# Routed experts with exact-split products: gate scaling on ScalarE, low weight parts on VectorE

## The chip, the cores and the metric

The kernel runs on one core of a Trainium2 chip. The metric is the device time of one execution in microseconds, as a median over runs. The core has five engines: PE (TensorE, matrix products), DVE (VectorE), ACT (ScalarE), POOL (GpSimd) and SP (SyncE, which here only issues DMAs). ACT and POOL issue DMAs too. Every engine works through its own instructions in their order.

## The reference, cut to what matters

Three layers follow each other over 2 x 768 tokens of width 512. The first is a retention attention of 8 heads. The second picks one of 8 experts for each token and scales the expert's output by its gate `p[e]`; the third is a gated layer with a convolution of three taps.

```python
# layer 2, for each token
h = np.maximum(x[b, s] @ w1[e], 0.0)
out[b, s] = p[e] * (h @ w2[e])
# layer 3
h = np.maximum(x @ w_in, 0.0)
conv_out += conv_w[k][None, None, :] * hp[:, k:k + S, :]
gate = 1.0 / (1.0 + np.exp(-conv_out))
return (h * gate @ w_out).astype(np.float32)
```

Inputs are float32 but for the third layer's weights, which the kernel decodes from 64 bit.

## The kernel before, in words

**Split products.** Each large product is computed as three float32r products, high x high, high x low and low x high. A weight piece of 128 x 1024 is called a unit. `split_first` (L180) has ACT round it to `whi` (L186); `split_second` (L189) has an engine that its caller names compute `wlo = raw - whi` (L194), and then has SP issue the load of a further unit into the freed `raw` buffer (there are four). `whi` and `wlo` have ten buffers each, so `whi` of a new unit waits until PE has used up an old one. 64 units belong to the experts. Eight more are the third layer's weights (`wdec`); the default of `split_unit` (L198) gives the low parts of the last four of these to POOL.

**Decoding.** `dec_first` and `dec_second` (L258, L272) decode the third layer's weights between the experts, 16 pieces in all: ACT reads the loaded piece `draw` (L226, L227), DVE does five operations (L229 to L235), POOL two (L237, L238), then the load of another piece is issued, on POOL's queue in the experts' loop (L255).

**The order around the change** is the order in which the code is written (a manual schedule), engine by engine. The stages are:

- The attention over twelve chunks, until about 91 us. Eight units are split here, on DVE.
- `alone(0, 0)`: the first 128 rows of expert 0, mixed with the end of the routing (`route_blocks`, `route_rest`); two units are split by a call at L831. `T(0, (1,))` (L638 to L644) transposes the second 128 rows: PE, then ACT (`xsh`), then DVE (`xsl`, L644).
- `alone(0, 1)`: the other rows of expert 0; two units are split by L715 and four by the default.
- Experts 1 to 6: `L1(e)` (first product, L763; ACT `hh` L768, DVE `hl` L769), `T(e + 1)`, one or two units by the default, `L2(e)` (second product, L792). `L1` splits a unit behind each of its steps `dt` = 0, 1 and 2 (L774) and finishes a decoding at `dt` = 0 and starts one at `dt` = 2. `L2` splits a unit behind each of its four steps `j` (L796), finishes a decoding at `j` = 1 and starts one at `j` = 3.
- Expert 7 in two halves (`alone(7, 0)`, `alone(7, 1)`). In the second half the outputs of batch 0 are gathered by index (`c_gather`, POOL's indirect DMA, tiles `yg`), scaled by the gate (`c_scale`, L989) and transposed and split (`c_T`: PE L995 into `x2p`, ACT high part L1005, DVE low part L1008), between the steps of the product L729.
- `moe2`: `h2(c, f0, f1)` computes groups of 12 products (L1038) into one of three PSUM banks. `conv` takes a bank through ACT `hs` (L1052) and `cs` (L1055), DVE `cs` twice (L1057), ACT `sg` (L1061), POOL `sg` (L1062), ACT `gh` (L1066) and DVE `gl` (L1067). `o2(c)` computes the output products (L1090), ACT copies them out (L1104). Between `h2(0)` and the four groups of `h2(1, 0, 4)` stand the six scalings of batch 1.

Of the kernel before, what the change touches and what calls it, by code (L numbers as in the profile page):

```python
# [13 lines left out]
AF = mybir.ActivationFunctionType  # L14
ALU = mybir.AluOpType
# [79 lines left out]
def tile_kernel(ctx: ExitStack, tc: tile.TileContext, consts, q, k, v, w_gate, w_local, w1, w2, w_in, conv_w, w_out, out):  # L95
# [565 lines left out]
    def moe(mo):  # L661
# [25 lines left out]
        def alone(e, half, free):  # L687
# [16 lines left out]
            for f in range(2):  # L704
                pb = bank_b("l1t")
                fs = slice(f * 512, (f + 1) * 512)
                for dt in range(KD):
                    wh, wl = split[e * 8 + dt]
                    for n, (a, b_) in enumerate(((xh, wh), (xh, wl), (xl, wh))):
                        nc.tensor.matmul(pb, lhsT=a[:, dt, :], rhs=b_[:, fs], start=(dt == 0 and n == 0),  # L710
                                         stop=(dt == KD - 1 and n == 2))
                    if f and free:
                        split.pop(e * 8 + dt)
                        if dt % 2 == 0:
                            split_unit(nc.vector if e else nc.gpsimd)  # L715
                    if f and dt == 1:
                        back(0)
                    if dt < KD - 1:
                        yield
                hr[f] = mo.tile([P, 512], F32, name="hr", tag="ow", bufs=2)  # L720
                nc.scalar.activation(out=hr[f], in_=pb, func=AF.Relu)
                yield
# [25 lines left out]
        def L1(e):  # L748
            xh, xl = xs_t.pop(e)
            hh, hl = h_tiles(e)  # L750
            pb = [bank_b("l1") if j < 3 else bank_d("l1") for j in range(KF // 2)]
            for dt in range(KD):
                wh, wl = split[e * 8 + dt]
                if dt == 0:
                    dec_second(nc.gpsimd)
                elif dt == 2:
                    dec_first(mo)
                for ft in range(KF):
                    o = pb[ft // 2][:, (ft % 2) * CAP:(ft % 2 + 1) * CAP]
                    fs = slice(ft * P, (ft + 1) * P)  # L760

                    for n, (a, b_) in enumerate(((wh, xh), (wl, xh), (wh, xl))):
                        nc.tensor.matmul(o, lhsT=a[:, fs], rhs=b_[:, dt, :], start=(dt == 0 and n == 0 and ft % 2 == 0),  # L763
                                         stop=(dt == KD - 1 and n == 2), skip_group_check=True)
                    if dt == KD - 1 and ft % 2:
                        fp = ft // 2
                        dst = hh[:, 2 * fp:2 * fp + 2, :].rearrange("p a t -> p (a t)")
                        nc.scalar.activation(out=dst, in_=pb[fp], func=AF.Relu)  # L768
                        nc.vector.scalar_tensor_tensor(out=hl[:, 2 * fp:2 * fp + 2, :].rearrange("p a t -> p (a t)"),  # L769
                                                       in0=pb[fp], scalar=0.0, in1=dst.bitcast(F32), op0=ALU.max,  # L770
                                                       op1=ALU.subtract)
                split.pop(e * 8 + dt)
                if dt < KD - 1:
                    split_unit(nc.gpsimd if dt == 0 else nc.vector)  # L774

        def L2(e):
            hh, hl = h_t.pop(e)
            yp = [bank_c(f"y{t}") for t in range(2)]

            for j in range(KF // 2):  # L780
                wh, wl = split[e * 8 + KD + j]
                if j == 1:
                    dec_second(nc.gpsimd)
                elif j == 3:
                    dec_first(mo)
                for jj in range(2):
                    ft = 2 * j + jj
                    ws = slice(jj * DM, (jj + 1) * DM)
                    for part in (((hh, wh), (hh, wl)), ((hl, wh),)):
                        for t in range(2):  # L790
                            for a, b_ in part:
                                nc.tensor.matmul(yp[t], lhsT=a[:, ft, t * P:(t + 1) * P], rhs=b_[:, ws],  # L792
                                                 start=(ft == 0 and a is hh and b_ is wh),
                                                 stop=(ft == KF - 1 and a is hl))
                split.pop(e * 8 + KD + j)
                split_unit(nc.gpsimd if j == 0 else nc.vector)  # L796
            for t in range(2):
                ys = mo.tile([P, DM], F32, name="ys", tag="ys", bufs=2)
                nc.scalar.copy(ys, yp[t])
                r = YROW + e * CAP + t * P  # L800
                nc.scalar.dma_start(out=scr[r:r + P, :], in_=ys)
# [25 lines left out]
        for n, _ in enumerate(first):  # L827
            if n in (1, 4):
                next(blocks, None)
            if n in (3, 5):  # L830
                split_unit(nc.gpsimd)  # L831
            if n >= 5:
                next(rest, None)
            if n == 5:
# [151 lines left out]

    def c_scale(t):
        y = yg_t[t]
        nc.vector.tensor_scalar(y, y, G_all[:, t:t + 1], None, op0=ALU.mult)  # L989

    def c_T(b, c):
        y = yg_t.pop(b * NC + c)
# [259 lines left out]
```

## Time and profile before

| what | value |
|---|---|
| median of 3 runs | 463.89 us (463.18 to 464.21) |
| the profiled execution: its time | 462.48 us |
| its span, first to last instruction | 460.7 us |
| PE busy | 421.1 us, 91% |
| DVE busy | 318.1 us, 69% |
| ACT busy | 244.3 us, 53% |
| POOL busy | 212.3 us, 46% |

The profile is of one execution. Its span leaves out 1.78 us at the ends, and its time lies 1.41 us under the median. Positions such as "at 113.7" are microseconds from the start of the span. A row of the timeline has start and length, the engine, the line, what is written and read, how many instructions are merged, and in brackets how long the engine was idle before and what ended that. An instruction's length counts from its start at the engine and holds what it waits there for a port. Busy time of PE holds modelled ends, so for PE the idle gaps and the distances between starts say more than the share.

### The profile page before, as it was taken

The numbers are of one execution on the slowest core, as the hardware profiler recorded it, in microseconds if no ns is written. First come the engines' busy times: TensorE is split into PE (matmuls) and PEld (weight loads), VectorE is DVE, ScalarE is ACT, GpSimd is POOL, SyncE is SP. The second block draws the span as 40 slices with busy tenths as digits, with TensorE's granted clock in tenths as the row PEclk, the third lists the DMA queues.
The fourth block names the chain that finished last, engine by engine and source line by source line (L and its number), as shares of the span: only waits on it lengthen the run. The fifth ranks groups of instructions, "written<-read, shape, count | busy, mean of one in ns | idle before, by whom it ended". The sixth has DMA issues, their size and how long they took to land.

```text
span 460.7 us, 7610 instructions
## 1 busy us (share of the span) xinstructions
PE 421.1 (91%) x2899; PEld 366.3 (80%) x2899; DVE 318.1 (69%) x540; ACT 244.3 (53%) x450; POOL 212.3 (46%) x159
## 2 busy tenths in 40 slices
PE   7899788678999989899998989948998999999996
PEld 4888677555698978789897977738996988998986
DVE  3366888857398969596979887475897263896160
ACT  2445564523575666456565565336866344784341
POOL 4631263306446576757676755384654030353030
PEclk9999999999899999999999999988999999999999
DMA  9989995433386868677778631040220101000101
GB/s 194 216 219 278 303 256 182 143 135 115 113 299 229 287 228 296 219 276 249 275 236 301 238 138 48 29 132 23 68 70 21 49 0 63 7 2 2 68 0 70
DMA packets 56521, 70.00 MB, mean 152 GB/s; under 512 B 28693, under 2 KB 35349, under 8 KB 56482
## 3 DMA queue, kind: packets, MB, share of 16 engines
q1 hardware_dynamic: 45490, 45.75, 32.8%
q0 software_dynamic: 3856, 13.13, 9.0%
q10 hardware_dynamic: 7136, 10.60, 6.5%
q8 instruction: 24, 0.39, 0.3%
q14 instruction: 15, 0.12, 0.1%
HBM read 58.99 MB, written 10.49 MB: 151 GB/s over the span
## 4 chain that ended last, share of the span: by engine, by line
PE 34%; DVE 29%; DMA 14%; POOL 9%; ACT 6%; issue 6%; ACTq 0%; SPq 0%; POOLq 0%; DVEq 0%
PE op L1090 11%; PE h L1038 9%; DVE wlo L194 6%; DMA draw<-in_moe_w_out_dram 6%; POOL wdec L238 3%; POOL dmf L237 3%; DVE cs L1057 3%; DVE gl L1067 3%; DVE dmf L229 2%; DVE hl L769 2%; DMA draw<-in_moe_w_in_dram 2%; PE l1t L710 2%; DMA k<-in_k_dram 2%; DVE xsl L644 2%; ACT whi L186 2%
## 5 line engine op out<-in xcount | busy, mean ns | idle before, releaser
L194 DVE TENSOR_TENSOR wlo<-raw,whi 128x1024 fp32r<-128x1024 f32 x48 | 77.0, 1622 | 21.1 <-ACT whi L186 21.0
L186 ACT CAST whi<-raw 128x1024 fp32r<-128x1024 f32 x64 | 67.1, 1052 | 38.1 <-PE y L792 19.7
L1062 POOL TENSOR_TENSOR sg<-sg,hs 128x384 f32<-128x384 f32 x32 | 37.0, 1158 | 80.2 <-ACT sg L1061 80.1
L1057 DVE SCALAR_TENSOR_TENSOR cs<-hs,cw,cs 128x384 f32<-128x384 f32 x64 | 43.9, 687 | 28.9 <-ACT cs L1055 27.8
L763 PE MATMUL l<-xsl,whi 128*128 128x256 f32 x192 | 54.4, 283 | 0.0
L763 PE MATMUL l<-xsh,wlo 128*128 128x256 f32 x192 | 54.3, 283 | 0.0
L763 PE MATMUL l<-xsh,whi 128*128 128x256 f32 x192 | 54.3, 283 | 0.0
L194 POOL TENSOR_TENSOR wlo<-raw,whi 128x1024 fp32r<-128x1024 f32 x16 | 41.8, 2619 | 26.2 <-ACT whi L186 18.8
L1038 PE MATMUL h<-x,whi 128*128 128x386 f32 x256 | 51.2, 338 | 0.0
L1038 PEld LDWEIGHTS h<-x,whi 128*128 128x128 f32 x256 | 45.2, 189 | 0.2
L237 POOL TENSOR_TENSOR dmf<-dmf,ds 128x512 f32<-128x512 f32 x13 | 23.9, 1842 | 38.6 <-DVE ds L235 38.6
L1090 PE MATMUL op<-whi,gh 128*128 128x512 f32 (+1 forms) x104 | 39.7, 381 | 1.5 <-ACT os L1104 1.5
L792 PE MATMUL y<-whi,hh 128*128 128x512 f32 x96 | 38.6, 402 | 2.1 <-ACT hh L768 2.1
L1090 PE MATMUL op<-whi,gl 128*128 128x512 f32 (+1 forms) x104 | 39.4, 379 | 0.1
L1090 PE MATMUL op<-wlo,gh 128*128 128x512 f32 (+1 forms) x104 | 39.2, 377 | 0.0
L792 PE MATMUL y<-wlo,hh 128*128 128x512 f32 x96 | 38.1, 397 | 0.0
L763 PEld LDWEIGHTS l<-xsh,whi 128*128 128x128 f32 x192 | 36.8, 192 | 0.2
L763 PEld LDWEIGHTS l<-xsh,wlo 128*128 128x128 f32 x192 | 36.8, 192 | 0.2
L1067 DVE TENSOR_TENSOR gl<-sg,gh 128x384 fp32r<-128x384 f32 x32 | 33.8, 1055 | 4.6 <-ACT gh L1066 4.6
L763 PEld LDWEIGHTS l<-xsl,whi 128*128 128x128 f32 x192 | 36.8, 192 | 0.0
L792 PE MATMUL y<-whi,hl 128*128 128x512 f32 x96 | 30.5, 400 | 3.8 <-DVE hl L769 3.8
L1038 PE MATMUL h<-x,wlo 128*128 128x386 f32 x128 | 27.7, 337 | 0.0
(200 smaller groups left out, 950.0 us busy)
## 6 DMA issues: line engine op xcount, KB each, us to landing
raw<-in_moe_w_dram SPq DMA_DIRECT2D x64, 512.0 KB, 4.4
scr<-ys ACTq DMA_DIRECT2D x16, 256.0 KB, 3.2
draw<-in_moe_w_out_dram POOLq DMA_DIRECT2D x8, 512.0 KB, 4.8
q<-in_q_dram SPq DMA_DIRECT2D x12, 256.0 KB, 4.5
v<-in_v_dram SPq DMA_DIRECT2D x12, 256.0 KB, 4.8
k<-in_k_dram SPq DMA_DIRECT2D x11, 256.0 KB, 4.4
scr<-xo ACTq DMA_DIRECT2D x11, 256.0 KB, 3.6
out_dram<-os ACTq DMA_DIRECT2D x11, 256.0 KB, 2.0
```

Source lines behind the costliest of these rows:

```text
L186: nc.scalar.copy(hi, raw[u])
L194: engine.tensor_tensor(out=lo, in0=t, in1=hi.bitcast(F32), op=ALU.subtract)
L229: ve.tensor_scalar(mag, mag, F64_LOW, F64_HIGH, op0=ALU.max, op1=ALU.min)
L237: nc.gpsimd.tensor_tensor(out=f, in0=f, in1=s.bitcast(F32), op=ALU.mult)
L238: nc.gpsimd.tensor_tensor(out=out, in0=f, in1=a.bitcast(F32), op=ALU.add)
L763: nc.tensor.matmul(o, lhsT=a[:, fs], rhs=b_[:, dt, :], start=(dt == 0 and n == 0 and ft % 2 == 0), stop=(dt == KD - 1 and n == 2), skip_gr ...
L792: nc.tensor.matmul(yp[t], lhsT=a[:, ft, t * P:(t + 1) * P], rhs=b_[:, ws], start=(ft == 0 and a is hh and b_ is wh), stop=(ft == KF - 1 an ...
L1038: nc.tensor.matmul(pb[:, 0:WN], lhsT=split[u_in + dt][wi][:, fs], rhs=x_[dt // 2][:, dt % 2, :], start=(n == 0), stop=(n == 3 * KD - 1))
L1057: nc.vector.scalar_tensor_tensor(out=cs, in0=tap[j], scalar=cw[:, j, ft:ft + 1], in1=cs, op0=ALU.mult, op1=ALU.add)
L1062: nc.gpsimd.tensor_tensor(out=sg, in0=sg, in1=tap[1], op=ALU.mult)
L1067: nc.vector.tensor_tensor(out=gl, in0=sg, in1=gh.bitcast(F32), op=ALU.subtract)
L1090: nc.tensor.matmul(ops[t][:, 0:n_], lhsT=a[:, ts_], rhs=b_[:, ws], start=(ft == 0 and n == 0), stop=(ft == KF - 1 and n == 2))
```

## The change

The five edits name another engine. Four calls of `split_unit` that gave the low part to POOL now give it to DVE: L715 (expert 0 alone had POOL), L774 (`dt` = 0), L796 (`j` = 0) and L831. `c_scale` is now an ACT activation with a scale taken from a column of `G_all`.

```diff
@@ alone, L715
-                            split_unit(nc.vector if e else nc.gpsimd)
+                            split_unit(nc.vector)
@@ L1, L774
-                    split_unit(nc.gpsimd if dt == 0 else nc.vector)
+                    split_unit(nc.vector)
@@ L2, L796
-                split_unit(nc.gpsimd if j == 0 else nc.vector)
+                split_unit(nc.vector)
@@ between the steps of alone(0, 0), L831
-                split_unit(nc.gpsimd)
+                split_unit(nc.vector)
@@ c_scale, L989
-        nc.vector.tensor_scalar(y, y, G_all[:, t:t + 1], None, op0=ALU.mult)
+        nc.scalar.activation(out=y, in_=y, func=AF.Copy, scale=G_all[:, t:t + 1])
```

PE and SP have the same instructions in the same order as before. On DVE in `alone(0, 0)`, where the block counts (L599 to L603) and the rows of the gathered outputs (L613) are computed:

```order
 L602 SCALAR_TENSOR_TENSOR inc<-nb,small_zero 128x8
 L603 CAST novi<-inc 128x1
+L194 TENSOR_TENSOR wlo<-raw,whi 128x1024
 L613 TENSOR_TENSOR rows<-OH,C 128x96
 L614 TENSOR_REDUCE posf<-rows 128x12
```

A low part now stands ahead of L613; another stands ahead of L599.

On DVE in experts 1 to 6, behind the two `xsl` of `T(e + 1)` and into `L2` (the five operations from L229 on are a decoding), before:

```order
L644 TENSOR_TENSOR xsl<-xsp,xsh 128x4x128 x2
L194 TENSOR_TENSOR wlo<-raw,whi 128x1024 x2
L229 TENSOR_SCALAR dmf<-dmf 128x512
L230 TENSOR_SCALAR dmf<-dmf 128x512
L232 TENSOR_SCALAR ds<-draw 128x512
```

and now:

```order
L644 TENSOR_TENSOR xsl<-xsp,xsh 128x4x128 x2
L194 TENSOR_TENSOR wlo<-raw,whi 128x1024 x3
L229 TENSOR_SCALAR dmf<-dmf 128x512
L230 TENSOR_SCALAR dmf<-dmf 128x512
L232 TENSOR_SCALAR ds<-draw 128x512
```

The low part of the unit split at `j` = 0 stands ahead of the decoding. It stood on POOL, ahead of L237, and is gone from there, as is the one of `L1` behind the load of `draw`.

On ACT in `alone(7, 1)`, where ACT has the high parts of the decoded weights (L186) and of the transposed outputs (L1005):

```order
 L701 CAST hh<-hTp 128x4x128
+L989 ACTIVATE yg_3598<-yg_3598,G_all 128x512
 L186 CAST whi<-wdec_84 128x1024
+L989 ACTIVATE yg_3598<-yg_3598,G_all 128x512
+L989 ACTIVATE yg_3599<-yg_3599,G_all 128x512
 L1005 CAST x_3608<-x2p 128x2x128
 L1005 CAST x_3609<-x2p 128x2x128
 L186 CAST whi<-wdec_85 128x1024
```

Three scalings now stand on ACT ahead of the first pair of L1005; three more follow between the later ones.

On ACT between `h2(0)` and `h2(1, 0, 4)`:

```order
 L1061 ACTIVATE sg<-cs 128x384
 L1066 CAST gh<-sg 128x384
+L989 ACTIVATE yg<-yg,G_all 128x512 x6
 L1052 ACTIVATE hs_3786<-h_4005 128x386
 L1055 ACTIVATE cs<-hs_3786,cw 128x384
```

The six scalings of batch 1 stand ahead of the `hs` that empties the ninth group's bank.

## Rows read from the trace of the kernel before

**Rows 1.** Stretches, experts 1 and 3, sum of six: length, busy by engine, clock.

```profile
130.86:154.19 23.33, 23.33 (x153) 21.40 (x152) 20.33 (x25) 13.92 (x20) 12.29 (x8) 1.00 0.78 284
...
179.40:206.63 27.23, 25.34 (x153) 22.27 (x152) 21.65 (x24) 14.85 (x21) 18.95 (x12) 0.94 0.72 244
...
sum 148.85, PE 142.97 PEld 129.07 DVE 125.70 ACT 88.26 POOL 94.44; mean PE 23.83 PEld 21.51 DVE 20.95 ACT 14.71 POOL 15.74
```

**Rows 2.** Timeline of PE, expert 3: first product of L2 behind a gap.

```profile
193.84 0.50 PE L792 MATMUL y<-whi,hh 128*128 128x512 f32 x1 [1.89 <-ACT hh L768]
```

**Rows 3.** Chain that ended last, around expert 5's L2: start, length, what.

```profile
240.97 2.92 DVE wlo L194
...
248.74 2.56 DVE dmf L229
...
257.74 6.10 DMA draw<-in_moe_w_out_dram
```

**Rows 4.** Timeline of POOL, then DVE, in the same place.

```profile
240.50 2.42 POOL L194 TENSOR_TENSOR wlo<-raw,whi 128x1024 fp32r<-128x1024 f32 x1
...
247.94 3.06 POOL L194 TENSOR_TENSOR wlo<-raw,whi 128x1024 fp32r<-128x1024 f32 x1 [1.76 <-ACT whi L186]
...
258.80 0.41 DVE L229 TENSOR_SCALAR dmf<-dmf 128x512 f32<-128x512 f32 x1
```

**Rows 5.** Low parts by engine: count, shortest/median/longest in ns.

```profile
L194 DVE TENSOR_TENSOR wlo<-raw,whi x48: 1207/1222/3040, 43.6 to 278.1; 128x1024 fp32r<-128x1024 f32 x48
L194 POOL TENSOR_TENSOR wlo<-raw,whi x16: 2372/2440/3062, 109.6 to 272.9; 128x1024 fp32r<-128x1024 f32 x16
```

**Rows 6.** Timelines at 107 to 116 (DVE, POOL, ACT, PE); stretch with its clock.

```profile
109.20 5.24 DVE L613 TENSOR_TENSOR rows<-OH,C 128x96 f32<-128x96 f16 x1
...
109.57 4.74 POOL L194 TENSOR_TENSOR wlo<-raw,whi 128x1024 fp32r<-128x1024 f32 x2
...
107.28 1.99 ACT L186 CAST whi<-raw 128x1024 fp32r<-128x1024 f32 x2
...
115.59 0.50 PE L710 MATMUL l1t<-whi,xsl 128*128 128x512 f32 x1 [1.85 <-DVE xsl L644]
...
116.00:119.60 3.60, 3.60 (x11) 2.57 (x10) 1.78 (x9) 0.66 (x2) 0.00 (x0) 0.53 0.50 190
```

**Rows 7.** Timelines at 305 to 321 (DVE, POOL, PE, ACT).

```profile
304.98 5.45 DVE L989 TENSOR_SCALAR yg<-yg,G_all 128x512 f32<-128x512 f32 x1 [1.56 <-DMA yg<-scr,posi]
...
305.50 4.64 POOL L194 TENSOR_TENSOR wlo<-wdec,whi 128x1024 fp32r<-128x1024 f32 x2
...
311.25 1.09 PE L995 MATMUL x2p<-C,yg 128*128 128x128 f32 x4 [6.22 <-DVE x L1008]
...
318.89 0.33 ACTq L742 DMA_DIRECT2D scr<-ys  x1
...
318.43 2.40 POOL L194 TENSOR_TENSOR wlo<-wdec,whi 128x1024 fp32r<-128x1024 f32 x1 [0.96 <-ACT whi L186]
...
319.94 0.76 DVE L1008 TENSOR_TENSOR x<-x2p,x 128x256 fp32r<-128x256 f32 x2 [1.49 <-ACT x L1005]
...
321.12 0.49 ACT L1052 ACTIVATE hs<-h 128x386 f32<-128x386 f32 x1 [1.21 <-DMA scr<-ys]
```

**Rows 8.** Timelines at 317 to 356 (PE, ACT, PE).

```profile
317.41 0.77 PE L1038 MATMUL h<-x,whi 128*128 128x386 f32 x3
...
339.25 0.49 ACT L1052 ACTIVATE hs<-h 128x386 f32<-128x386 f32 x1
...
342.69 0.39 PE L1090 MATMUL op<-whi,gh 128*128 128x512 f32 x1
...
355.51 0.50 PE L1090 MATMUL op<-whi,gh 128*128 128x512 f32 x1 [1.46 <-ACT os L1104]
```

**Rows 9.** Groups on ACT: count, busy us and mean ns, idle before.

```profile
L1055 ACT ACTIVATE cs<-hs,cw 128x384 f32<-128x384 f32 x32 | 19.8, 618 | 1.0
...
L1005 ACT CAST x<-x2p 128x256 fp32r<-128x256 f32 x24 | 7.9, 375 | 16.3 <-DVE x L1008 8.0 <-PE x2p L995 8.0 <-ACT ys L740 0.4
```

## The prediction

> **What bounds the kernel now.** PE is the busiest engine, so I read what PE waits for, stage by stage, and then who makes it wait. First the stretches of experts 1 to 6, each from the first product of one L1 to that of the next [rows 1]. Each expert has the same products. Expert 1 takes 23.33 us with PE busy throughout; that is PE's own pace. The six together take 148.85, which is 148.85 - 6 x 23.33 = 8.9 us more than this pace. Expert 3 is the longest with 27.23, and its mean clock is 0.94.
>
> Then PE's gaps [rows 2]. The largest one stands where L1 of expert 3 ends and L2 begins: PE waits 1.89 for `hh`; three other experts have gaps at the same place, for `hl`. Then the chain of waits, to see who is late [rows 3]. It runs in a loop: a piece `draw` lands, ACT reads it and rounds a unit, DVE takes 2.92 for one low part, then come `hl`, `xsl`, another low part, 2.56 for one L229, the rest of the decoding, POOL's two operations, and the next load of `draw`, which needs 6.10. ACT stands in its order behind that landing, and so do `hh` and, behind the low part, `hl`.
>
> Two lengths in that loop are far too long. A low part needs 1.22 at the median on DVE [rows 5], an undisturbed L229 needs 0.41 [rows 4]. The timeline of POOL tells why: its low part runs from 240.50 to 242.92, and DVE's, which started at 240.97, ends about 1.1 after that. The next one of POOL runs from 247.94 to 251.00, and DVE's L229 ends at 251.3 [rows 3, 4]. So DVE operations like these two, which read their tensors from SBUF, and POOL's exclude each other: one waits until the other is through.
>
> The same is seen at two more places. At 109.20 DVE's L613, 96 elements wide, takes 5.24 because POOL does two low parts from 109.57 on for 4.74; `xsl` stands behind it, PE waits 1.85, and then runs 3.6 us with the clock at 0.53, the lower of the two levels (1.2 GHz) for nearly all of it [rows 6]. At 304.98 a scaling on DVE takes 5.45 behind two low parts of POOL (4.64), and PE waits 6.22 [rows 7]. After the experts PE has one larger gap more, 1.46 at 355.51 [rows 8]; from there to the end it works through.
>
> **The change, part by part.** The rows below are from the profiled execution (462.48, span 460.7), so the sum is made on it; its 1.41 under the median is kept as an offset.
>
> *The two low parts in `alone(0, 0)`.* POOL's 4.74 go. DVE does them in its own order, 2 x 1.22. Their high parts are ready at 109.27 at the latest [rows 6]. DVE then has, from 108.3: a low part to 109.5, five counting operations of some 0.2 (my estimate from their width; they are no wider than L613), the second low part to about 111.7, L613 without the lock some 0.3, three small ones, and `xsl` by about 113. PE asks for it at 113.74, which is 115.59 - 1.85. So the gap goes, and with it the stretch at the low clock, 3.6 x (1 - 0.53) = 1.7. Term A: 1.85 + 1.7 = 3.5 us; bounds 0 (if something else delays `xsl` as much) and 3.6.
>
> *The twelve low parts in experts 1 to 6.* Each costs DVE 1.22 instead of POOL 2.44, so the pair has 1.2 less to share for each. In the loop the one of L1 no longer blocks DVE's last low part: 2.92 becomes 1.22, a saving of 1.7. The one of L2 now stands ahead of the decoding: 2.56 becomes 1.22 + 0.41 = 1.63, a saving of 0.9. The loop takes some 24.8 now: experts 2 to 6 take (148.85 - 23.33)/5 = 25.1 each, of which 27.23 x 0.06/5 = 0.3 is expert 3's clock. It comes to 24.8 - 2.6 = 22.2. That is under PE's 23.33, so PE sets the pace. The extra low part in L1 lies in a stretch where DVE waits for ACT, and costs nothing as long as DVE has 1.2 us there: it is busy 20.33 of 23.33 in expert 1, its waits for POOL included, and 20.33 + 2 x 1.22 = 22.8 still fits. The freed `raw` buffers are released earlier, because they no longer stand behind L237, L238 and the issue of `draw` on POOL; SP's loads follow them. Expert 3's gap is the one with `hh` last: it hangs on the landing of `draw` alone, which comes 0.9 earlier, so 1.0 of 1.89 stays, and I keep 0.4 for `hl` behind it. Term B: 8.9 - 1.4 = 7.5 us. Bounds: 8.9, and 2 if the loads of `draw`, now issued among other loads, land later and give the rest back.
>
> *The first six scalings, on ACT.* No scaling of this size is seen on ACT. The nearest row is L1055, the same form over 384 columns, 0.62; for 512 columns the bounds are 0.62 and 0.62 x 512/384 = 0.82, and I take 0.7, between them. The Trainium skill ("Perfetto Trace Analysis", Optimizing Scalar/DVE Operations) speaks against this edit: an operation that both engines can do is faster on DVE where a performance mode exists, and ACT is for when DVE is saturated. By that rule the sum would lose 12 x 0.2 us here; the trace differs at 304.98, where the scaling on DVE takes 5.45. On ACT the third scaling can start when its gather has landed, at 304.96 to 304.98 [rows 7]. POOL keeps the four low parts of decoded weights, but no scaling stands behind them. The DVE low parts L1008 read PSUM and one tensor in SBUF; these are not blocked now: a pair at 319.94 takes its usual 0.76 while POOL's low part runs from 318.43 to 320.83 [rows 7]. PE then no longer waits 6.22, and ACT becomes the limit of this stage. From 305.0 it has four scalings (2.8), three high parts of 1.0 [rows 6], ten casts L1005 at 7.9/24 = 0.33 [rows 9], some 0.5 for four very small ones and 0.4 for `ys`: 10.0. So the store of `ys` is issued at 315.0 instead of 318.89, 3.9 earlier, and the first `hs` of the third layer, which waits for that store [rows 7], starts 3.9 earlier.
>
> *The second six scalings, on ACT.* DVE loses them, but ACT gets 6 x 0.7 = 4.2 exactly ahead of the ninth `hs`, now at 339.25 [rows 8]. That `hs` frees the bank for PE's twelfth group (three banks). It would start at 339.25 - 3.9 + 4.2 = 339.55 and end at 340.04. The twelfth group starts now at 342.69 - 2.11 = 340.58 (twelve groups from 317.41, where the stage starts, to 342.69), so it starts 0.5 earlier than now, and PE, which is 3.5 or more ahead by then, waits about 3 us. Such a gap is followed by the low clock (1.85 was), which costs another 1.7. The 48 products from 342.69 then end about 1.2 later than now, in the place of the gap of 1.46, which goes. Term C: 0.3 us gained, or 2.0 if the clock stays up; I take 1.0. Bounds: 4, if ACT is quicker than counted, and -3.6, if the stage before gains nothing (4.2 - 0.85 of slack + 1.7 - 1.46).
>
> Sum: 3.5 + 7.5 + 1.0 = 12.0. Span 448.7, profiled execution 450.5, median 463.9 - 12.0 = **451.9**.
>
> **The rivals.** *The loads decide.* The loop's largest piece is the landing of `draw`, 6.10; if it grows by some 1.5 us for each expert because the weight loads move into it, the loop stays at 24 and term B shrinks to 2 to 3. For it: DMA is busy 0.72 to 0.78 in these stretches [rows 1]. Against it: it is the same number of bytes, and expert 1 keeps PE's pace with 0.78. Time 451.9 + 5 = 457.
>
> *ACT pays for the scalings.* ACT becomes the bound from 305 to 355, the first six scalings gain nothing there, and the second six cost what was worked out: C is -3.6, A and B stand. For it: ACT would stand in its order behind three landings of gathers, and a scaling of 0.7 is longer than one of some 0.5 on DVE. Against it: 6.22 us of idle PE that no longer have a cause. Time 451.9 + 4.6 = 456.5. This is what the rule quoted above from the Trainium skill ("Perfetto Trace Analysis", Optimizing Scalar/DVE Operations) would lead one to expect.
>
> *Slower: DVE behind a late high part.* In L2 DVE now waits for `whi` of `j` = 0 before it decodes, and that `whi` waits for PE to free a buffer. On POOL such a wait held back only POOL (1.76 at 247.94 [rows 4]). The loop is lengthened by whatever `whi` comes later than DVE's `xsl` and low part. It has 23.3 - 22.2 = 1.1 to spare. The kernel is slower as a whole once terms A and C (4.5) are used up too: the experts then take 8.9 + 4.5 = 13.4 more than PE's pace, 2.7 for each of five, and `whi` is 1.1 + 2.7 = 3.8 late in each. At 6 us late the loop takes 28.2 and the time is 463.9 - 4.5 + 5 x 4.9 - 8.9 = 475. In the rows POOL's low part starts at 247.94, before DVE is through with its own (248.7), so `whi` is early, and this is unlikely.
>
> *It doesn't do what it says.* Not all low parts leave POOL: those of the last four decoded units stay, two of them in the 4.64 at 305.50. If the lock held DVE's L1008 too, the gap of 6.22 would stay and term C be -3.6: 456.5.
>
> **How the numbers follow.** The forecast (all three terms near their values) 0.66; loads 0.16; ACT pays 0.08; L1008 locked 0.05; slower 0.05. The best case is 3.6 + 8.9 + 4 = 16.5 gained, 447.4; the range goes from 447.0 to 458.0, which takes in the forecast and most of the three middle cases. A measurement can tell about 0.2% (0.9 us) from no change. Faster by more than that: 0.93, as all but the slower case lie well under 463; within 0.2%: 0.02; slower 0.05.
>
> **What would show it.** A right: L613 under 0.5 and no low clock at 116. B right: each of the six stretches at 23.3 to 24, L229 at 0.4, DVE's low parts near 1.2 with at most an operation of POOL (1.3) in front. B wrong: ACT's L226 still waits for `draw` by 2 us and more. C right: scalings on ACT of 0.6 to 0.8, no gap of 6 us near 305, and a new wait of PE for ACT's `hs` in the twelfth group of L1038. The forecast is wrong if the stretches of the experts stay at 24.9.

## The result, and the profile after

The changed kernel takes 451.07 us (median of 4 runs, 450.61 to 451.4) where the kernel before, run beside it, takes 464.05 (463.18 to 464.6). The ratio is 0.972, interval 0.970 to 0.974: 13.0 us, 2.8%. The forecast was 451.9 with a range of 447.0 to 458.0. The profiled execution took 451.4, its span is 448.9. A run more than 1.5% above the fastest of its kernel counts as slow and is left out where kernels are compared.

I cut both spans at the same products of PE and compare stage by stage (distances between starts, read off PE's timeline):

| stage | before | after | difference | forecast |
|---|---|---|---|---|
| start to the first transposition of `T(0, (1,))` | 109.44 | 111.54 | +2.10 | 0 |
| from there to the first product of expert 1 | 21.42 | 18.65 | -2.77 | A: -3.5 |
| experts 1 to 6 | 148.85 | 139.90 | -8.95 | B: -7.5 |
| start of `alone(7)` to the 49th product of L1090 | 75.80 | 73.74 | -2.06 | C: -1.0 |
| from there to the end | 105.18 | 105.09 | -0.09 | 0 |
| span | 460.69 | 448.92 | -11.77 | -12.0 |

**Who sets the end.** The page's fourth part, the chain of work that ended last, in shares of the span, of before and then of after:

```profile
PE 34%; DVE 29%; DMA 14%; POOL 9%; ACT 6%; issue 6%; ACTq 0%; SPq 0%; POOLq 0%; DVEq 0%
...
PE 59%; ACT 5%; DVE 5%; issue 2%; DMA 2%; POOL 0%; POOLq 0%; ACTq 0%; DVEq 0%
```

**The experts.** The stretches of after that answer to [rows 1], experts 1 and 3 and the sum of six (length, busy by engine, clock, DMA share, GB/s):

```profile
130.19:153.50 23.31, 23.31 (x153) 21.40 (x152) 21.88 (x27) 13.84 (x20) 9.85 (x7) 1.00 0.83 274
...
176.82:200.13 23.31, 23.31 (x153) 21.40 (x152) 21.29 (x25) 14.56 (x20) 13.29 (x10) 1.00 0.80 277
...
sum 139.90, PE 139.90 PEld 128.40 DVE 118.12 ACT 87.96 POOL 68.33; mean PE 23.32 PEld 21.40 DVE 19.69 ACT 14.66 POOL 11.39
```

Expert 3, which took 27.23, now has PE's own pace like the others; the sum of PE's busy time is the sum of the stretches. DVE has twelve low parts more in them and is busy 118.12 instead of 125.70: what it lost in waits is more than what it took over. The low parts and the first step of a decoding, over the whole kernel (count, shortest/median/longest in ns), which answer to [rows 4, 5]:

```profile
L194 DVE TENSOR_TENSOR wlo<-raw,whi x64: 1210/1223/2324, 44.0 to 266.7; 128x1024 fp32r<-128x1024 f32 x64
L229 DVE TENSOR_SCALAR dmf<-dmf x13: 414/420/423, 132.3 to 278.8; 128x512 f32<-128x512 f32 x13
```

The longest L229 is 0.42 now; it was 2.56 in [rows 3]. The longest low part of DVE is 2.32, not 3.04: it waits 1.1 for a POOL operation of the decoding, no longer for a low part.

**Expert 0.** First a row of before, DVE's copy `ys` (L739); then the timelines of DVE and PE of after, where [rows 6] stood:

```profile
117.25 0.36 DVE L739 COPY ys<-y 128x256 f32<-128x256 f32 x1
...
112.38 1.23 DVE L194 TENSOR_TENSOR wlo<-raw,whi 128x1024 fp32r<-128x1024 f32 x1
113.52 0.25 DVE L613 TENSOR_TENSOR rows<-OH,C 128x96 f32<-128x96 f16 x1
...
114.18 0.69 DVE L644 TENSOR_TENSOR xsl<-xsp,xsh 128x512 fp32r<-128x512 f32 x1
...
116.59 0.36 DVE L739 COPY ys<-y 128x256 f32<-128x256 f32 x1
...
118.82 0.50 PE L710 MATMUL l1t<-whi,xsh 128*128 128x512 f32 x1 [0.77 <-ACTq L885]
```

Two stretches of the same place with their clock, the 1.00 ahead of DMA share and GB/s:

```profile
115.00:118.00 3.00, 2.92 (x12) 2.17 (x12) 2.04 (x11) 0.66 (x2) 0.21 (x1) 1.00 0.53 179
118.00:122.00 4.00, 3.23 (x17) 2.57 (x16) 1.10 (x1) 2.78 (x5) 1.68 (x2) 1.00 0.63 196
```

L613 falls from 5.24 to 0.25, `xsl` is there in time, PE's gap of 1.85 is gone, and the clock stays at its upper level (2.4 GHz). But a wait of 0.77 is new, at L885, where the engines read the count of overflow blocks and branch. PE's own branch is long past by then (113.1); it waits until ACT has passed (118.8). ACT comes there behind its store of `ys`, and so behind DVE's L739.

**The scalings.** The timelines of ACT (the third and the fourth scaling) and POOL from 293 on, then of ACT and PE at 325; they answer to [rows 7, 8]:

```profile
293.48 0.72 ACT L989 ACTIVATE yg<-yg,G_all 128x512 f32<-128x512 f32 x1 [0.58 <-DMA yg<-scr,posi]
...
295.58 0.73 ACT L989 ACTIVATE yg<-yg,G_all 128x512 f32<-128x512 f32 x1
...
294.85 4.69 POOL L194 TENSOR_TENSOR wlo<-wdec,whi 128x1024 fp32r<-128x1024 f32 x2
...
306.69 0.49 ACT L1052 ACTIVATE hs<-h 128x386 f32<-128x386 f32 x1 [1.10 <-DMA scr<-ys]
...
324.80 3.78 ACT L989 ACTIVATE yg<-yg,G_all 128x512 f32<-128x512 f32 x6
...
329.01 1.66 PE L1038 MATMUL h<-x,whi 128*128 128x386 f32 x4 [2.56 <-ACT hs L1052]
```

And the stretch behind PE's gap, with its clock of 0.64:

```profile
328.20:332.90 4.70, 3.89 (x14) 3.85 (x15) 3.19 (x5) 4.19 (x10) 1.28 (x2) 0.64 0.00 0
```

The third scaling takes 0.72 instead of 5.45, but it is over before POOL's pair of low parts begins. The fourth and the fifth run beside that pair (294.85 to 299.54) and take 0.73 and 0.74: on ACT they are not held. PE's gap of 6.22 has become gaps of 1.36, 0.76 and 0.86. The six scalings ahead of the ninth `hs` take 3.78, and PE waits 2.56 for that `hs` in the twelfth group.

**Ahead of every edit.** The 2.10 that after loses before 111 is in no term. Two stretches of after show the lower clock (1.2 GHz) there:

```profile
90.00:93.00 3.00, 3.00 (x30) 2.48 (x26) 2.93 (x6) 0.47 (x3) 1.65 (x2) 0.50 0.97 332
100.00:104.00 4.00, 3.99 (x14) 2.72 (x14) 0.52 (x2) 0.92 (x3) 0.00 (x0) 0.57 0.00 0
```

In the profile of before both read 1.00. The instructions are the same up to 110.3, where the first moved low part starts. Not all of the 2.10 is the clock: 0.38 was there by 84, ahead of both stretches. Across the first stretch only 0.07 is added, since PE waited there for 1.43 in before and doesn't now. Across the second, from the product L570 at 99.42 in before (100.01 in after) to the next one of that line, it is 1.40. The last pair of experiments returns to this.

### The profile page after: what moved, and what is told of

It reads as the page before. It is cut to its first block, busy times and chain, and to the rows that moved or that the text cites. A ratio compares the mean times of both kernels' runs of the same rounds, so it can differ in the third digit from the quotient of the medians.

```text
span 448.9 us, 7625 instructions
## 1 busy us (share of the span) xinstructions
PE 420.4 (94%) x2899; PEld 367.5 (82%) x2899; DVE 297.8 (66%) x544; ACT 251.6 (56%) x462; POOL 175.6 (39%) x143
## 4 chain that ended last, share of the span: by engine, by line
PE 59%; ACT 5%; DVE 5%; issue 2%; DMA 2%; POOL 0%; POOLq 0%; ACTq 0%; DVEq 0%
PE l L763 15%; PE y L792 15%; PE op L1090 13%; PE h L1038 9%; PE y L729 2%; DVE cs L1057 2%; DVE gl L1067 2%; PE l1t L710 1%; ACT yg L989 1%; PE xsp L641 1%; DMA scr<-ys 1%; DMA yg<-scr,posi 1%; ACT cs L1055 1%; ACT x L1005 1%; ACT hs L1052 1%
## 5 line engine op out<-in xcount | busy, mean ns | idle before, releaser
L194 DVE TENSOR_TENSOR wlo<-raw,whi 128x1024 fp32r<-128x1024 f32 x64 | 86.8, 1373 | 24.4 <-ACT whi L186 24.3
L186 ACT CAST whi<-raw 128x1024 fp32r<-128x1024 f32 x64 | 66.5, 1054 | 34.6 <-PE y L792 17.4
L237 POOL TENSOR_TENSOR dmf<-dmf,ds 128x512 f32<-128x512 f32 x13 | 26.5, 2042 | 82.7 <-DVE ds L235 59.8
L1038 PE MATMUL h<-x,whi 128*128 128x386 f32 x256 | 52.3, 343 | 2.6 <-ACT hs L1052 2.6
L1090 PE MATMUL op<-whi,gh 128*128 128x512 f32 (+1 forms) x104 | 39.6, 381 | 0.0
L1090 PE MATMUL op<-whi,gl 128*128 128x512 f32 (+1 forms) x104 | 39.4, 379 | 0.1
L1090 PE MATMUL op<-wlo,gh 128*128 128x512 f32 (+1 forms) x104 | 39.2, 377 | 0.0
L792 PE MATMUL y<-whi,hl 128*128 128x512 f32 x96 | 29.6, 389 | 0.0
L669 POOL DMA_INDIRECT xg<-scr,permi x15 | 17.9, 1194 | 25.7 <-ACT hr L721 16.3
```

The costliest lines, as they stand in the source:

```text
L186: nc.scalar.copy(hi, raw[u])
L194: engine.tensor_tensor(out=lo, in0=t, in1=hi.bitcast(F32), op=ALU.subtract)
L237: nc.gpsimd.tensor_tensor(out=f, in0=f, in1=s.bitcast(F32), op=ALU.mult)
L669: nc.gpsimd.indirect_dma_start(out=t, out_offset=None, in_=xrow, in_offset=bass.IndirectOffsetOnAxis(ap=permi[:, col:col + 1], axis=0))
L1038: nc.tensor.matmul(pb[:, 0:WN], lhsT=split[u_in + dt][wi][:, fs], rhs=x_[dt // 2][:, dt % 2, :], start=(n == 0), stop=(n == 3 * KD - 1))
L1090: nc.tensor.matmul(ops[t][:, 0:n_], lhsT=a[:, ts_], rhs=b_[:, ws], start=(ft == 0 and n == 0), stop=(ft == KF - 1 and n == 2))
```

## The experiments

The theory is the prediction's: low parts on POOL lengthen DVE operations, these lengthen the loop through the landing of `draw` and the order of `alone(0, 0)`, and the scalings on ACT are a small part. The main rival is that the scalings carry the gain, or that the loads do. The runs stand on several chips, on which the kernel before has medians of 463.3 to 464.05; a difference from the changed kernel's 451.07 holds to about 0.8.

### One half of the change at a time

Low parts on DVE, the scaling left there:

```diff
-        nc.scalar.activation(out=y, in_=y, func=AF.Copy, scale=G_all[:, t:t + 1])
+        nc.vector.tensor_scalar(y, y, G_all[:, t:t + 1], None, op0=ALU.mult)
```

> The low parts on DVE as in the changed kernel, the twelve scalings left on DVE as before. Theory (three places that add up: the beginning 2.8, the experts' loop 8.9, the scalings 2.1 us): the six stretches of the experts 139.9 in sum, L613 under 0.5, but the third scaling again some 5 us behind POOL's two low parts of decoded weights and PE's gap of 6 us still there; 464.0 - 11.7 = 452.3 us. Rival (the scalings carry the gain, the low parts only move it): 460 or more. Rival (the parts need each other, because a DVE relieved of the scalings is what makes room): stretches of 142 to 146 and 455 to 458.

Measured: 450.86 (450.48 to 451.91), ratio 0.971 (0.967 to 0.975), no different from the whole change. The stretches sum to 141.64, not 139.9 as expected; the time was 1.4 better than expected. The lock is still there for one scaling; timelines of DVE, POOL and PE:

```profile
294.46 0.49 DVE L989 TENSOR_SCALAR yg<-yg,G_all 128x512 f32<-128x512 f32 x1 [1.32 <-DMA yg<-scr,posi]
295.86 4.89 DVE L989 TENSOR_SCALAR yg<-yg,G_all 128x512 f32<-128x512 f32 x1 [0.24 <-DMA yg<-scr,posi]
...
295.78 4.67 POOL L194 TENSOR_TENSOR wlo<-wdec,whi 128x1024 fp32r<-128x1024 f32 x2
...
301.55 1.09 PE L995 MATMUL x2p<-C,yg 128*128 128x128 f32 x4 [4.47 <-DVE x L1008]
```

The third scaling slips in ahead of POOL's pair in 0.49, the fourth arrives 0.08 after the pair's start and takes 4.89. The stage from `alone(7)` to the 49th product of L1090 is 73.24, against 75.80 before and 73.74 with the whole change: there the low parts alone bring as much as the whole change. But no low part of that stage was moved; what differs is when POOL's pair falls against the scalings. In the run below without the loads of `draw`, all low parts are on POOL, and the stage reads 74.49, its gap 4.51.

The scaling on ACT, with all low parts as before (the one line of L989 in the kernel before):

> Only the scalings on ACT, all low parts as before. Theory: the stretches of the experts stay at 148.9 in sum; PE's gap of 6 us near 305 goes, in its place three gaps under 1.5; PE waits 2.5 us for ACT's ninth hs and then runs at the lower clock; 464.0 - 2.1 = 461.9 us. Rival (ACT pays for the scalings): 464 to 468. Rival (the scalings carry the gain): 454 or less.

Measured: 462.35 (459.78 to 464.69), ratio 0.997 (0.995 to 1.000). The stretches of the experts, as a sum:

```profile
sum 149.23, PE 143.12 PEld 129.32 DVE 120.75 ACT 88.23 POOL 93.95; mean PE 23.85 PEld 21.55 DVE 20.12 ACT 14.71 POOL 15.66
```

PE's timeline at the ninth `hs`:

```profile
341.43 1.65 PE L1038 MATMUL h<-x,whi 128*128 128x386 f32 x4 [2.56 <-ACT hs L1052]
```

The experts stay where they were. The gap of 6.22 goes, gaps of 1.43, 0.78, 0.45 and 1.83 come in its place, and 2.56 at the ninth `hs`. By the medians the scalings alone are worth about 1 us, as term C had it; the interval reaches 1.000, so no gain at all isn't excluded.

### The three places of the low parts

The changed kernel with the low part of `L1`'s `dt` = 0 back on POOL:

```diff
@@ L774
-                    split_unit(nc.vector)
+                    split_unit(nc.gpsimd if dt == 0 else nc.vector)
```

> The changed kernel with the low part behind dt = 0 of L1 back on POOL (six of the sixteen). Theory (a loop through the landing of draw, 24.8 us before, PE's pace 23.3): this one blocks DVE's last low part ahead of hl, so the loop loses 1.7 of the 2.6 saved and takes 23.9 to 24.1; experts 2 to 6 take 0.6 to 0.8 more each, the sum of the stretches is 143 to 144, the time 451.1 + 3 to 4 = 454 to 455 us. Rival (every low part on POOL costs the pair of DVE and POOL the same): 451.1 + 8.9/2 = 455.5. Rival (only the throughput of DVE counts, which gets less work): no change, 451.

Measured: 457.6 (453.28 to 458.13), ratio 0.983 (0.976 to 0.990): a miss in size, and more so in form. Three of the four runs lie at 457.1 to 458.1, the fourth at 453.28. The stretches of experts 1 and 2 and the sum:

```profile
128.19:151.50 23.31, 23.31 (x153) 21.40 (x152) 17.64 (x23) 12.81 (x17) 8.74 (x6) 1.00 0.74 240
151.50:181.25 29.75, 26.22 (x153) 23.13 (x152) 24.81 (x28) 16.80 (x24) 17.57 (x12) 0.89 0.76 261
...
sum 146.37, PE 142.84 PEld 130.06 DVE 117.47 ACT 88.46 POOL 75.69; mean PE 23.81 PEld 21.68 DVE 19.58 ACT 14.74 POOL 12.61
```

The timelines of SP, ACT, DVE and POOL around the end of expert 1:

```profile
139.86 4.20 SPq L177 DMA_DIRECT2D raw<-in_moe_w_dram  x4
...
147.88 1.05 ACT L186 CAST whi<-raw 128x1024 fp32r<-128x1024 f32 x1 [3.20 <-DMA raw<-in_moe_w_dram]
...
148.96 1.23 DVE L194 TENSOR_TENSOR wlo<-raw,whi 128x1024 fp32r<-128x1024 f32 x1 [3.03 <-ACT whi L186]
...
156.99 0.61 POOL L255 DMA_DIRECT2D draw<-in_moe_w_in_dram  x1
```

I expected 0.6 to 0.8 more in each of five experts; expert 2 has all of it (6.4) and the four behind it keep PE's pace. The form is that of the prediction's slower rival, at one place: DVE waits 3.03 for the `whi` of `j` = 0 with the decoding behind it, and the load of `draw` is issued 5.5 after the start of the next L1 (151.50); in the changed kernel it is 1.3. But `whi` isn't late because PE frees its buffer late, as that rival has it. ACT waits 3.20 for a load of `raw`. SP issues these loads from 139.86 on, 11.7 after the start of L1, when POOL's low part (137.06 to 139.83) has freed the buffer; that low part stands behind L237, L238 and the issue of `draw`. In the changed kernel they begin 5.7 after it. This is what term B had said of the `raw` buffers, the other way round. Of the 6.4, 3.5 are PE's two gaps at the start of L2 (1.49 and 2.04), and 2.9 the lower clock behind them (PE is busy 26.22 instead of 23.31). The run of 453.28 is hardly one with such an expert.

The same for the low part of `L2`'s `j` = 0:

```diff
@@ L796
-                split_unit(nc.vector)
+                split_unit(nc.gpsimd if j == 0 else nc.vector)
```

> The changed kernel with the low part behind j = 0 of L2 back on POOL (six of the sixteen). Theory of the loop: it loses 0.9 of the 2.6 saved and takes 23.1, still under PE's pace of 23.3; the sum of the stretches stays at 140 to 140.5, the time at 451.1 to 451.6 us. Rival (every low part on POOL costs the same): 455.5 us with stretches of 144.4 in sum.

Measured: 454.71 (453.09 to 454.86), ratio 0.978 (0.974 to 0.983): a miss, 3 us more than I expected. The sum of the stretches:

```profile
sum 142.98, PE 141.43 PEld 128.12 DVE 131.28 ACT 87.57 POOL 84.08; mean PE 23.57 PEld 21.35 DVE 21.88 ACT 14.60 POOL 14.01
```

The timelines of DVE and POOL in expert 3:

```profile
195.46 2.62 DVE L229 TENSOR_SCALAR dmf<-dmf 128x512 f32<-128x512 f32 x1
...
194.76 3.04 POOL L194 TENSOR_TENSOR wlo<-raw,whi 128x1024 fp32r<-128x1024 f32 x1 [3.09 <-ACT whi L186]
```

POOL's 3.04 makes L229 2.62, as in [rows 3, 4]; the load of `draw` is issued 2.3 to 4.1 after the starts of L1 of experts 2 to 6 (1.2 to 2.7 in the changed kernel), and four of the stretches are longer, expert 3's by 1.85. In the profile 3.1 of the loss against the changed kernel lies in the experts; behind `alone(7)`, where nothing was edited, it loses 1.6 more, and ahead of the edits it is 0.9 shorter. With either one back, experts 4 to 6 take 70.0 and 70.8 (69.95 in after, 73.1 before). So the two savings don't add: taking one low part out of the loop brings these three near PE's pace. Runs with this stage untouched read 139.9 to 141.6 (in one of them expert 4 took 24.11), so of these 3.1 only 1.4 lies outside what such runs differ by.

The two low parts of `alone(0, 0)` back on POOL:

```diff
@@ L831
-                split_unit(nc.vector)
+                split_unit(nc.gpsimd)
```

> The changed kernel with the two low parts at the beginning (L831) back on POOL. Theory: L613 takes about 5 us again, PE waits some 1.7 us for xsl and may run at the lower clock after it; from the first transposition of expert 0's second half to L1(1) 21.3 us instead of 18.7, so the span is 2.7 longer, 453 to 454.5 us. Rival (the experts' weights come no earlier, so the gain at the beginning is lost again in experts 1 to 3): 451, with longer stretches in the changed kernel than here.

Measured: 453.55 (453.45 to 454.28), ratio 0.980 (0.978 to 0.983): 2.5 above the changed kernel. PE's timeline there, at its two gaps:

```profile
116.84 0.50 PE L710 MATMUL l1t<-whi,xsl 128*128 128x512 f32 x1 [1.84 <-DVE xsl L644]
...
120.78 0.50 PE L710 MATMUL l1t<-whi,xsh 128*128 128x512 f32 x1 [1.38 <-ACTq L885]
```

The stretch for which [rows 6] show a clock of 0.53, here with 1.00:

```profile
116.00:119.60 3.60, 2.57 (x10) 1.80 (x10) 3.01 (x14) 0.66 (x2) 1.63 (x2) 1.00 0.81 269
```

The gap of 1.84 is back, as large as in [rows 6], but this time the clock stays up. The stage is 21.45 long all the same, as before with the low clock (21.42): PE gets to the products behind L885 earlier and waits there for 1.38 instead. What sets the stage is DVE's L739, which stands behind L613. From the first transposition it starts 7.81 later in before, 7.83 here and 5.05 in after; the first product that waits for L885 follows after 10.13 (with no wait left), 10.05 and 7.28. So the stage gains what DVE gains, 2.8, and the low clock of [rows 6] cost at most 0.1.

### The loop without its landing

The kernel before, with 11 of the 16 loads of `draw` left out (the decoding takes a piece that is already there):

```diff
+        if u >= 5:
+            dec_raw[u] = dec_raw["kept"][u % 2]
+            return
...
+        dec_raw["kept"] = dec_raw.get("kept", [None])[-1:] + [t]
```

> The kernel before, without the loads of draw in the experts' loop: eleven of the sixteen pieces of the third layer's weights are not loaded, and decoded from two pieces loaded earlier; all work of the engines stays, the low parts stay on POOL. Theory (the loop goes through the landing of draw, 6 us of 24.8): without it PE sets the pace although DVE and POOL block each other as before; the stretches come to 140 to 142 in sum instead of 148.9, the time to 455 to 457 us. Rival (DVE and POOL together are too slow for PE's pace, whatever the loads do): stretches of 147 to 149, 462 to 464 us.

Measured: 454.77 (453.19 to 455.21), ratio 0.981 (0.978 to 0.984). All low parts are on POOL as before; the stretch of expert 3 and the sum:

```profile
178.86:203.59 24.73, 23.83 (x153) 21.35 (x152) 21.00 (x27) 15.42 (x21) 17.93 (x10) 1.00 0.64 229
...
sum 141.32, PE 140.42 PEld 128.35 DVE 112.25 ACT 88.84 POOL 92.44; mean PE 23.40 PEld 21.39 DVE 18.71 ACT 14.81 POOL 15.41
```

7.5 of the experts' 8.9 go although every low part stays on POOL: the loop needs the loads of `draw` to cost PE that much. The run doesn't hold the lock fixed, though. DVE is busy 112.25 instead of 125.70 with the same operations, so its waits for POOL were shorter. It also moves fewer bytes (expert 3 has a DMA share of 0.64 instead of 0.72), so that the wait for the landing and the traffic of the loads aren't told apart here; that the landing is the link is read from the chain in [rows 3].

### Where the scalings belong

The changed kernel with the first six scalings on ACT and the second six on DVE:

```diff
-        nc.scalar.activation(out=y, in_=y, func=AF.Copy, scale=G_all[:, t:t + 1])
+        if t < NC:
+            nc.scalar.activation(out=y, in_=y, func=AF.Copy, scale=G_all[:, t:t + 1])
+        else:
+            nc.vector.tensor_scalar(y, y, G_all[:, t:t + 1], None, op0=ALU.mult)
```

> The changed kernel, with the first six scalings on ACT and the second six back on DVE. Theory (the first six gain some 5 us in front of the third layer, the second six give most of that back as PE's wait of 2.6 us for ACT's ninth hs and the lower clock after it): no such wait and no low clock at its place, from the first hs to the 49th product of L1090 34.4 us as in the kernel before instead of 37.1, hence 2.5 to 2.8 us faster than the changed kernel: span near 446.2, time 448 to 449 us. Rival (the second six cost nothing, PE would have waited 1.4 us at L1090 anyway and something else sets the pace): 451, as the changed kernel.

Measured: 446.6 (445.95 to 448.15), ratio 0.966 (0.963 to 0.969), below both kernels and below the forecast. Three lines are added, so L992, L1093 and L1107 here are L989, L1090 and L1104 elsewhere. The timelines of DVE, at the second six, and of PE, at its only gap over 0.4 behind the start of the third layer:

```profile
324.09 3.07 DVE L992 TENSOR_SCALAR yg<-yg,G_all 128x512 f32<-128x512 f32 x6
...
338.97 0.50 PE L1093 MATMUL op<-whi,gh 128*128 128x512 f32 x1 [1.29 <-ACT os L1107]
```

The wait for the ninth `hs` is gone. The stage from `alone(7)` to the 49th product of L1090, with the low parts of raw units on DVE:

| first six | second six | stage |
|---|---|---|
| DVE | DVE | 73.24 |
| ACT | ACT | 73.74, in a second profile 72.78 |
| ACT | DVE | 70.94, in a second profile 70.89 |

So the first six on ACT gain 2.3, and the second six there take 1.9 to 2.8 back. The first row is one profile. With all twelve on ACT three more profiles, of the experiments on the low parts, read 73.7 to 75.4; only the last row is below all others. The rule that the prediction quoted from the Trainium skill ("Perfetto Trace Analysis", Optimizing Scalar/DVE Operations) holds in one half and fails in the other: six scalings take 3.07 on DVE and 3.78 on ACT where POOL has no low part; beside POOL's low parts DVE needs 4.89 for one. That section also says that POOL shares an SBUF read port with DVE, which fits.

Then POOL was cleared: all low parts on DVE, those of the last four decoded units too (the default of `split_unit`), with all scalings on DVE, with the split as above, and with the first six alternating between ACT and DVE:

```diff
-            split_second(engine or (nc.vector if nxt["split"] <= n_dram + KD else nc.gpsimd))
+            split_second(nc.vector)
```

> All low parts on DVE, those of the last four decoded units too, and all scalings on DVE. Theory (the 5 us of a scaling are a wait for POOL's low parts and nothing else): every scaling takes 0.4 to 0.5, PE has no gap over 2 us near 300, the third layer starts as early as with the scalings on ACT or earlier, and the second six cost DVE 3 us as before: 1 to 4 us faster than the kernel with only the low parts changed (450.9), so 447 to 450 us. Rival (the scaling waits for its gather, and POOL's low parts only stand beside it): one scaling of several us or a wait for yg in its place, 451.

> The version with only the first six scalings on ACT (446.6, its gaps in alone(7, 1) 1.36, 0.77, 0.45 and 1.82), and in addition the four low parts of decoded weights on DVE too, so that POOL has no low part at all. Theory (ACT is what PE waits for in that stage; POOL's low parts no longer block anything there, because the scalings have left DVE and L1008 reads PSUM): the gaps stay, within 0.5 us of 446.6. Rival (POOL's low parts, 2.4 each, still come late for the first products of the third layer): 445 or less, with the first product of L1038 earlier by 1 us or more.

> As the run before (all low parts on DVE, second six scalings on DVE), but the first six scalings alternate: ACT has those of chunks 0, 2 and 4, DVE those of 1, 3 and 5. Theory (ACT's queue sets alone(7, 1)): ACT loses 3 x 0.62 = 1.9 there, DVE without POOL's lock needs 0.48 for each, and the gaps of 4.6 us in sum fall to about 2.7: 444.7. Rival (a scaling on DVE then stands behind low parts or behind L1008 in DVE's order, as in the run with everything on DVE, whose gaps there sum to 5.1): 446.5 to 447.5.

Measured: 450.82 (449.68 to 451.19), 450.07 (449.13 to 453.76) and 450.63 (449.43 to 454.16). All three are misses. The first came out at its rival's time, though its theory was right about the scalings; the other two lie 3.5 and 4.0 above the plain split's 446.6 (2.8 and 3.4 above its second measurement below). ACT's timeline of the first, at the copy `ys` whose store the first `hs` waits for:

```profile
305.94 0.37 ACT L740 COPY ys<-y 128x256 f32<-128x256 f32 x1 [1.70 <-DVE ys L739]
```

And of the second, with DVE's:

```profile
302.87 1.05 ACT L186 CAST whi<-wdec 128x1024 fp32r<-128x1024 f32 x1
...
304.03 1.23 DVE L194 TENSOR_TENSOR wlo<-wdec,whi 128x1024 fp32r<-128x1024 f32 x1 [0.26 <-ACT whi L186]
305.17 0.42 DVE L739 COPY ys<-y 128x256 f32<-128x256 f32 x1
...
305.62 0.37 ACT L740 COPY ys<-y 128x256 f32<-128x256 f32 x1 [1.70 <-DVE ys L739]
```

In the first a scaling on DVE takes 0.48 at the median and 1.09 at most, never 4.9, so what held it was POOL's low part. But the last decoded low part stands ahead of DVE's `ys` (L739), and itself waits for ACT's `whi` of 302.87. ACT then waits 1.70 for DVE, and the first `hs` starts 38.6 to 38.8 after the start of `alone(7)` instead of 36.6. On POOL the same wait holds nobody. In the alternating version PE's gaps over 0.4 before the third layer sum to 6.0 instead of 4.4.

### The split against the changed kernel

Both kernels once more, in one comparison on one chip:

> The changed kernel once more, on the chip of the next run, to set the two against each other. Both theories: 450.6 to 451.4, with the wait of 2.56 for the ninth hs.

> The version with the first six scalings on ACT and the second six on DVE once more, beside the changed kernel. Its first measurement lay 4.5 below the changed kernel's, of which its profile puts 2.8 behind the start of alone(7) and 2.2 ahead of expert 0's second half, where nothing was edited and the clock was down in the changed kernel's profile at 90 to 93 and 100 to 104. Theory (the clock ahead of the edits comes and goes between executions): the medians differ by 2.3 to 3.3 here. Rival (the edit as a whole is worth it): 4.5 again, and xsp of expert 0's second half at 109.3 in this profile and at 111.5 in the other.

Measured: 449.39 for the changed kernel (five runs, 447.73 to 452.0; with the sixth, 455.98, the median is 450.27) and 447.28 for the split (446.93 to 450.12), ratios to the kernel before 0.972 (0.969 to 0.976) and 0.968 (0.965 to 0.970). The medians differ by 2.1, just under the expected 2.3 to 3.3 and not by 4.5; the two ranges overlap, so the order rests on the stage too, 72.78 against 70.89. And the changed kernel's second profile has a span of 445.9 instead of 448.9. Its stretches, to be set against 90 to 104 and 328.2 to 332.9 of the first:

```profile
90.00:93.00 3.00, 1.24 (x19) 0.91 (x15) 2.46 (x6) 1.59 (x3) 0.92 (x1) 1.00 0.78 299
100.00:104.00 4.00, 4.00 (x23) 2.87 (x22) 1.23 (x6) 0.90 (x4) 0.00 (x0) 1.00 0.00 0
94.00:97.00 3.00, 3.00 (x14) 2.59 (x12) 2.24 (x8) 1.08 (x4) 0.00 (x0) 0.53 0.75 244
326.50:331.50 5.00, 4.09 (x21) 3.73 (x22) 3.39 (x6) 4.49 (x10) 1.47 (x2) 1.00 0.00 0
```

The clock is up in the three places where it was low, but low from 94 to 97, where it costs 0.4 against before. The transposition that stood at 111.54 stands at 109.41, and the gap for the ninth `hs` is still 2.57. So the 2.10 ahead of the edits is a difference between executions of one program. All fourteen profiles agree: that product stands at 109.3 to 109.6 in the six that have at most one such stretch between 88 and 105, and at 110.6 to 111.5 in the eight that have more of the lower clock there.

## Why the prediction was right, point by point

**The bound: right.** PE's pace was there to be had, and the way to it was DVE operations stretched by POOL's low parts. Putting the low part of `L2` or of `L1` back makes the kernel 3.6 or 6.5 slower, of which 3.1 and 6.5 lie in the experts in the profiles; taking the loads of `draw` away from the kernel before gives most of term B. One thing in the rows doesn't fit as told: L613 and the scaling at 304.98 start 0.37 and 0.52 before POOL's pairs by the record, and undisturbed (0.25 and 0.48) they would have been over by then. What held them in that time is not shown.

**Term A: cause right, path wrong.** 2.8 by the stretches, 2.5 by the runs, for 3.5. L613 was freed and PE's gap of 1.85 went as worked out. But the sum 1.85 + 1.7 is not what was gained. The step that failed is that I followed PE only through its gap and the slow stretch behind it, and not to its next wait. That is the wait for ACT to pass L885, behind DVE's L739 and so behind L613. The 1.7 for the clock was nothing (0.1 at most): with the two low parts back on POOL the gap came again, the clock stayed up, and PE lost the same time at L885. The stage gained 2.77 because DVE came to L739 2.76 earlier.

**Term B: right, size too small.** 8.95 for 7.5; the bound of 8.9 was the value. The 1.4 that I kept for expert 3, because `draw` would still land late for `hh`, was not there: PE has no gap in it. ACT still waits for `draw`, by 3.89 once and under 2 otherwise, before L226, but nothing behind it on PE is late. By the prediction's own sign for "B wrong", a wait of L226 of 2 us and more, term B would have failed at that place; so that was no sign of it. The loop's arithmetic (24.8 - 1.7 - 0.9) gave the sign, not the parts: with one of its two savings undone the loss was 3.1 at most, 1.85 of it in expert 3, in one case, and 6.4 in a single expert in the other, by a late load of `raw` that the loop's arithmetic doesn't hold. In these runs the loop, near its limit, did not slip by the same amount in each turn.

**Term C: the two halves right, their sum by luck.** The first half was forecast as a first `hs` 3.9 earlier against the start of the stage; it is 4.8 earlier (41.41 to 36.60), of which 2.55 comes with the low parts alone and 1.9 with the loads of `draw` left out alone, by when POOL's pair falls. For the second half I had a wait of about 3 in the twelfth group and a low clock: 2.56, and a clock of 0.64 in one profile and 1.00 in another. The rule behind that (a gap like 1.85 is followed by the low clock) was already against a row of before: its gap of 2.03 at 89.00 is followed by a clock of 1.00. A scaling on ACT is 0.72, inside 0.62 to 0.82; six in a row overlap to 3.78 where I had 4.2. The term was 2.1 in one profile and 3.0 in the other, for 1.0. But the edit for which it stands, the scaling on ACT, is worth nothing measurable on top of the low parts (450.86 without it): what I booked to it would have come anyway, and its second half was a loss that a split avoids.

**The sum.** The stages gained 13.8 where I had 12.0, and the profiled execution gave 2.1 of it back ahead of all edits, 1.4 of that by its clock at 100 to 104. The median fell by 13.0. That the forecast lies 0.8 above the result is in part such cancelling.

**The rivals.** The loads did not decide: the DMA share rises to 0.80 to 0.83 in experts 1 to 5 and the stretches stay at 23.3. ACT does pay, 1.9 to 2.8, for the second six only. L1008 was not blocked beside POOL. The slower rival did not occur in the changed kernel, but a late `whi` ahead of the decoding is real: it cost 6.4 in expert 2 when the low part of `L1` went back to POOL, there behind a late load and not behind PE.

## What to carry to other kernels

Where a DVE operation has several times its undisturbed length, look at POOL's timeline in the same microseconds: moving POOL's operation to DVE can make DVE less busy. Follow a saving to the next wait of the same engine before it is booked, and undo one part of a loop at a time before its savings are added. Place an operation by what stands behind it in its queue: six scalings were a gain on ACT at one place and a loss at another, and the four low parts that can wait were better left on POOL.

## What had not been expected of the hardware

The lower clock does not follow each gap of PE. After the same gap of 2.02, which begins at 86 to 87, the stretch from 90 to 93 has a clock of 0.50 in one profile of the changed kernel and 1.00 in the other, where it is low a little later, 0.53 from 94 to 97. A gap of 1.85 before `xsl` was followed by 0.53 in [rows 6], one of 1.84 by 1.00; the gap of 2.56 for the ninth `hs` by 0.64, one of 2.57 by 1.00. What decides was not found out.

Nor does a slow stretch have one price. It cost 1.4 at 100 to 104, where PE has no wait to give, 0.4 at 94 to 97, and 0.1 or less at 90 to 93 and at 116, where PE would have waited anyway. A price of 1.7 behind every gap is too certain twice over. One program's spans differ by 3.0 (448.9 and 445.9); 0.8 of that stands there by 84, 1.3 more comes up to the first transposition with the clock, and 1.0 between the start of `alone(7)` and the 49th product of L1090.
